# A row-packed two-head attention with 0/1 masks, and a circular convolution in half-length transforms, on one Trainium2 core

## The chip, the core and the metric

The kernel runs on one core of a Trainium2 chip. Its engines are TensorE (PE, whose weight loads are listed apart as PEld), VectorE (DVE), ScalarE (ACT), GpSimd (POOL) and SyncE (SP), which here only issues DMAs. Each engine runs its own instructions in order; semaphores tie them together. The metric is the device time of one launch in microseconds.

## The reference

Four batches, eight heads, 768 positions, 64 values a head. Three of the heads ("retrieval") see all earlier positions, the others only the first four positions and a window of 64. The output of all heads, 512 wide, goes through a gate: two projections multiply a third one that was convolved along the sequence (circularly, by FFT) with a filter given over time.

```python
scores = scale * np.matmul(q, k.transpose(0, 1, 3, 2))
stream_keep = causal & (is_sink | in_win)
mask = np.where(retr[0, :, 0, 0, None, None], full_mask, stream_mask)
scores = np.where(mask[None, :, :, :], scores, -1000000000.0)
a = np.exp(scores - np.max(scores, axis=-1, keepdims=True))
a = a / (np.sum(a, axis=-1, keepdims=True) + 1e-09)
x = np.matmul(a, v)                      # heads side by side: (B, S, 512)
proj = x @ w_proj                        # x1, x2, x3
X2 = np.fft.rfft(x2, n=S, axis=1)
H = np.fft.rfft(filter_fft, n=S, axis=0)[None, :, :]
x2_conv = np.fft.irfft(X2 * H, n=S, axis=1)
return (x1 * x2_conv * x3) @ w_out
```

## The kernel before

The work goes over 16 pairs of heads, four to a batch; the sequence is cut into six blocks of 128. `emit_loads` fetches q, k and v of a pair on SP's queue, two pairs ahead. `emit_prep` casts them to bf16 on DVE, transposes q and k on PE (L248, L250) and brings them back: q as two tiles qT_A and qT_B, each with one head's 64 rows and zeros in the other 64 (GpSimd memsets, L254 and L255), kT by a copy on ACT (L259).

`emit_attention` computes the scores transposed, keys down and queries across. For each head and key block a matmul of up to 512 columns fills one PSUM tile sc (four buffers; L275), a second one with the identity adds the mask to the first 256 columns (L284), and one exponential with a bias per head writes pT (L291). The value products (L306) take each 128x128 block of pT as weights against v with a column of ones, and DVE divides by that column (L313, L314). `flush_store` transposes the result into xT_all (L325, L327).

The gate of a batch is `emit_moe_proj` (x1 and x3, which are multiplied into g, L355 to L370; x2, L376, L382) and `emit_moe_fft`: a forward transform, a product with a 768x768 matrix G_all of cosines and sines (Xa L393, Xb L399), the complex product with the filter's transform Hp_all on DVE (L408 to L416), the inverse with G's transpose Minv_all (dps, L423), the product with g (L429), and the output projection (L434, copied on ACT, L441, stored on SP). Its PSUM tiles share two buffers.

G_all is built in twelve chunks by `emit_dft_chunk`, two in each of the first six pairs: angles on PE, their remainders on ACT and DVE, a sine on ACT (L220). Minv_all, six transposed tiles, is built in pairs 6 to 8, and Hp_all (`emit_hp`, L333, L339) after pair 8. The loop at the end writes prep of the next pair, one such step, attention, store and, after a batch's fourth pair, the gate; the first gate's transform waits until pair 8. The code order gives priorities only: a scheduler merges these streams on each engine by dependencies, buffers and its own estimate.

## Time and profile before

| | us |
|---|---|
| runs of the kernel, median of 3 | 390.17 (390.12 to 391.35) |
| span of the profiled execution | 390.7 |
| PE busy, share of the span | 298.7, 76% |
| ACT busy | 220.1, 56% |
| DVE busy | 177.3, 45% |
| POOL busy | 30.5, 8% |
| mean granted PE clock | 0.951 |

The profiled execution has no time of its own beside its span, which lies within the runs. Busy times of engines overlap, so none of them is the time by itself; a row of a group gives the mean of one instruction and, behind the second bar, how long its engine stood idle before it and whom it waited for. PE's mean includes the time in which a result is still on its way, so a dense run of matmuls is read from its length and count, not from the mean. A granted clock of 1.00 is 2.4 GHz, and the other level is 1.2 GHz; a figure between is a mix over the stretch.

### The profile page before, as it was taken

What the parts mean: (1) busy time and instruction counts of PE and PEld (TensorE: products, weight loads), DVE (VectorE), ACT (ScalarE), POOL (GpSimd) and SP (SyncE); (2) the same over time, 40 slices, a digit from 0 to 9 for tenths busy, and PEclk for the clock granted to TensorE, in tenths of its full rate; (3) what the DMA queues carried; (4) which work ended last, traced back from release to release, by engine and by line L of the source; (5) the groups of instructions that cost most, each with busy time, mean ns of one, the idle gap of its engine ahead of it and who ended that gap; (6) DMA issues with size and microseconds to landing.
All of it is one profiled execution on the core that took longest, in us unless ns stands there. A gap on an engine that the chain in (4) does not pass through costs nothing.

```text
span 390.7 us, 5920 instructions
## 1 busy us (share of the span) xinstructions
PE 298.7 (76%) x2257; PEld 176.7 (45%) x2288; DVE 177.3 (45%) x411; ACT 220.1 (56%) x409; POOL 30.5 (8%) x51
## 2 busy tenths in 40 slices
...
GB/s 148 198 197 225 83 154 59 81 42 120 2 122 3 29 94 49 124 112 81 3 41 2 81 169 114 2 168 75 2 0 2 1 142 23 0 2 0 0 2 161
DMA packets 80732, 28.44 MB, mean 73 GB/s; under 512 B 75840, under 2 KB 77120, under 8 KB 80704
## 3 DMA queue, kind: packets, MB, share of 16 engines
...
q14 instruction: 10, 0.08, 0.1%
...
## 4 chain that ended last, share of the span: by engine, by line
PE 51%; ACT 27%; DVE 7%; SPq 6%; DMA 4%; issue 4%; ACTq 0%; DVEq 0%
ACT pT L291 13%; PE dps L423 8%; PE sc L275 7%; PE x2p L376 5%; PE x3p L362 4%; ACT L291 4%; PE Xa L393 4%; ACT L220 4%; PE attout L306 4%; PE Xb L399 4%; PE x1p L355 3%; SPq L109 3%; PE ops L434 3%; DMA out_dram<-o_sb 3%; PE sc L284 3%
## 5 line engine op out<-in xcount | busy, mean ns | idle before, releaser
L291 ACT ACTIVATE pT<-sc,bias_all 128x512 bf16<-128x512 f32 (+3 forms) x256 | 120.2, 563 | 40.3 <-PE sc L284 24.6
L275 PE MATMUL sc<-qT_B,kT 128*128 128x512 bf16 (+3 forms) x128 | 41.1, 341 | 27.7 <-ACT pT L291 26.0
L306 PE MATMUL attout<-v_aug,pT 128*128 128x65 bf16 x672 | 54.0, 207 | 5.2 <-ACT pT L291 5.0
L306 PEld LDWEIGHTS <-pT 128*128 128x128 bf16 x672 | 41.8, 107 | 35.6 <-issue 19.2
L284 PE MATMUL sc<-mask_all,identity 128*128 128x256 bf16 x192 | 53.8, 290 | 0.3 <-DVE bias_all L171 0.2
L275 PE MATMUL sc<-qT_A,kT 128*128 128x128 bf16 (+3 forms) x126 | 38.3, 325 | 11.5 <-ACT pT L291 8.4
L259 ACT COPY kT<-kT_ps 128x768 bf16<-128x768 bf16 x16 | 12.8, 800 | 53.6 <-PE kT_ps L250 53.6
L313 DVE RECIPROCAL rec<-attout 128x6 f32<-128x6 f32 x32 | 6.2, 193 | 74.0 <-PE attout L306 73.9
L441 ACT COPY o_sb<-ops 128x512 f32<-128x512 f32 x24 | 14.0, 588 | 41.3 <-PE ops L434 27.0
L423 PE MATMUL dps<-Minv_all,P_all 128*128 128x512 bf16 (+1 forms) x188 | 34.8, 324 | 1.9 <-DVE m L411 0.6
L275 PEld LDWEIGHTS <-kT 128*128 128x128 bf16 x256 | 26.7, 105 | 19.2 <-issue 4.7
L284 PEld LDWEIGHTS <-identity 128*128 128x128 bf16 x192 | 19.5, 102 | 32.6 <-issue 29.3
L248 PE MATMUL qT_ps<-identity,q_bf 128*128 128x128 bf16 x96 | 14.1, 246 | 25.3 <-DVE q_bf L237 25.3
L370 DVE TENSOR_TENSOR g_all<-x1s,x3p 128x512 bf16<-128x512 bf16 (+1 forms) x32 | 17.7, 554 | 26.5 <-PE x3p L362 17.5
L355 PE MATMUL x1p<-xT_all,wproj_bf 128*128 128x256 bf16 (+1 forms) x120 | 25.6, 322 | 3.3 <-DVE xT_all L327 1.7
L362 PE MATMUL x3p<-xT_all,wproj_bf 128*128 128x256 bf16 (+1 forms) x123 | 26.2, 323 | 2.0 <-DVE g_all L370 1.5
L369 ACT CAST x1s<-x1p 128x512 bf16<-128x512 f32 (+1 forms) x32 | 15.3, 479 | 18.9 <-PE x1p L355 18.8
L423 PEld LDWEIGHTS <-P_all 128*128 128x128 bf16 x192 | 18.4, 97 | 15.9 <-issue 2.7
L254 POOL MEMSET qT_A<- 64x768 bf16 x16 | 12.1, 757 | 169.2 <-PE sc L284 136.9
L429 DVE TENSOR_TENSOR y_all<-g_all,dps 128x512 bf16<-128x512 bf16 (+1 forms) x32 | 17.0, 554 | 14.2 <-PE dps L423 14.2
L434 PE MATMUL ops<-wout_bf,y_all 128*128 128x512 bf16 x93 | 21.8, 378 | 1.1 <-ACT o_sb L441 0.8
L376 PE MATMUL x2p<-wproj_bf,xT_all 128*128 128x512 bf16 x93 | 21.3, 379 | 0.2
...
## 6 DMA issues: line engine op xcount, KB each, us to landing
...
ret_i<-in_is_retrieval_dram SPq DMA_DIRECT2D x1, 8.0 KB, 3.8
```

Source lines behind the costliest of these rows:

```text
L220: nc.scalar.activation(out=G_all[:, tcn, a:b], in_=m2_f, func=AF.Sin, bias=sinb, scale=ETA)
L275: nc.tensor.matmul(sc, lhsT=kT[:, j * 128:(j + 1) * 128], rhs=qTh[:, j * 128 + a:j * 128 + bb], start=True, stop=(a != 0),)
L284: nc.tensor.matmul(sc[:, 0:mw], lhsT=identity, rhs=mask_all[:, h, midx, 0:mw], start=False, stop=True,)
L291: nc.scalar.activation(out=pT, in_=sc, func=AF.Exp, bias=bias_all[:, bias_idx:bias_idx + 1], scale=SCALE,)
L306: nc.tensor.matmul(attout[:, i, :], lhsT=pt_pieces[hh][j][piece][:, qloc:qloc + 128], rhs=v_aug[:, j, 65 * hh:65 * hh + 65], start=(j == 0 ...
L355: nc.tensor.matmul(x1p, lhsT=wproj_bf[:, cc, cb * 128:(cb + 1) * 128], rhs=xT_all[:, b, cc, a:bb], start=(cc == 0), stop=(cc == NC - 1),)
L362: nc.tensor.matmul(x3p, lhsT=wproj_bf[:, cc, 2 * DM + cb * 128:2 * DM + (cb + 1) * 128], rhs=xT_all[:, b, cc, a:bb], start=(cc == 0), stop ...
L370: nc.vector.tensor_mul(g_all[:, cb, a:bb], x1s, x3p)
L376: nc.tensor.matmul(x2p, lhsT=xT_all[:, b, cc, ti * 128:(ti + 1) * 128], rhs=wproj_bf[:, cc, DM:2 * DM], start=(cc == 0), stop=(cc == NC - 1),)
L423: nc.tensor.matmul(dps, lhsT=P_all[:, rc, cb * 128:(cb + 1) * 128], rhs=Minv_all[:, rc, a:bb], start=(rc == 0), stop=(rc == NT - 1),)
L429: nc.vector.tensor_mul(y_all[:, cb, a:bb], g_all[:, cb, a:bb], dps)
L434: nc.tensor.matmul(ops, lhsT=y_all[:, cb, ti * 128:(ti + 1) * 128], rhs=wout_bf[:, cb, :], start=(cb == 0), stop=(cb == NC - 1),)
```

## The change

**Scores.** q stays one tile qT with head A in rows 0 to 63 and head B in rows 64 to 127, as kT. Each score matmul takes 64 rows, the two heads in turn, into two halves of one sc tile of 2x512 columns (two such buffers, four banks). The 21 blocks on and below the diagonal are packed into five chunks of four and one of one (CHUNKS), so that a pair has six exponentials over both heads, with no bias.

**Masks.** The identity matmuls go. DVE multiplies the first two blocks of each chunk (diagonal and the one beside it) by 0/1 masks after the exponential. The blocks farther off use v_far, a copy of v and its ones column multiplied by 0 or 1 per key and head on GpSimd.

**Convolution.** The sequence is folded, first half plus second and first minus second: even frequencies need only the sum, odd ones only the difference, so each transform has 384 points. G holds three such row blocks of six column groups; the last two groups take half a tile each for even and odd frequencies (64 output columns of the array forward, 64 rows back). Angles are computed without PE, and the three sines stand in one place. The inverse gives an even part ev and an odd part od; their sum and difference are the two halves.

**Order and buffers.** kT comes back on DVE. qT, kT, x and the gate's tiles all use ps_m with two buffers; att has one. The gate is a generator whose stages are emitted between the next batch's pairs, so batch 0's gate starts beside pair 5; all of batch 3's and the end of batch 2's come behind pair 15.

```diff
+CHUNKS = [
+    [(0, 0), (0, 1), (0, 2), (0, 3)],
+    [(4, 4), (4, 5), (0, 4), (0, 5)],
+    [(1, 1), (1, 2), (1, 3), (1, 4)],
+    [(3, 3), (3, 4), (3, 5), (1, 5)],
+    [(2, 2), (2, 3), (2, 4), (2, 5)],
+    [(5, 5)],
+]
+PLACE = {ji: 4 * c + n for c, blocks in enumerate(CHUNKS) for n, ji in enumerate(blocks)}
+NBLK = 21
...
+    asb = ctx.enter_context(tc.tile_pool(name="att_sb", bufs=2))
+    pTp = ctx.enter_context(tc.tile_pool(name="att_pT", bufs=2))
+    psw = ctx.enter_context(tc.tile_pool(name="ps_w", bufs=2, space=bass.MemoryType.PSUM))
+    pso = ctx.enter_context(tc.tile_pool(name="ps_o", bufs=1, space=bass.MemoryType.PSUM))
+    mps = ctx.enter_context(tc.tile_pool(name="ps_m", bufs=2, space=bass.MemoryType.PSUM))
...
-         tc.tile_pool(name="att_ps_w", bufs=4, space=bass.MemoryType.PSUM) as psw, \
-         tc.tile_pool(name="att_ps_o", bufs=2, space=bass.MemoryType.PSUM) as pso, \
-         tc.tile_pool(name="moe_ps", bufs=2, space=bass.MemoryType.PSUM) as mps:
...
+    for h in range(H):
+        nc.vector.scalar_tensor_tensor(
+            out=mask[:, h], in0=only, scalar=ret[:, h:h + 1], in1=stream,
+            op0=ALU.mult, op1=ALU.add,
+        )
+    vmask = const.tile([128, H, 2], FP32, name="vmask")
+    nc.vector.tensor_copy(out=vmask, in_=ret[:, :, None].to_broadcast([128, H, 2]))
+    if n_sink:
+        nc.vector.memset(vmask[0:n_sink, :, 0], 1.0)
...
+    G = const.tile([128, NM, 6, 128], BF16, name="G")
+    for m in range(NM):
+        e_t = setup.tile([128, 6, 128], FP32, name="e_t", bufs=2)
+        nc.vector.scalar_tensor_tensor(out=e_t, in0=fcol, scalar=tcol[:, m:m + 1], in1=off,
+                                       op0=ALU.mult, op1=ALU.add)
+        n_t = setup.tile([128, 6, 128], I32, name="n_t", bufs=2)
+        nc.vector.tensor_scalar(out=n_t, in0=e_t, scalar1=1.0 / S, scalar2=None, op0=ALU.mult)
+        nc.vector.scalar_tensor_tensor(out=e_t, in0=n_t, scalar=-float(S), in1=e_t,
+                                       op0=ALU.mult, op1=ALU.add)
+        nc.scalar.activation(out=G[:, m], in_=e_t, func=AF.Sin, scale=ETA)
+    Gi = const.tile([128, 6, HS], BF16, name="Gi")
+    def emit_inverse_matrix():
+        for t in range(0, 6, 2):
+            ps = mps.tile([128, 2, HS], BF16, name="gi_ps", tag="m")
+            for u in range(2):
+                for m in range(NM):
+                    nc.tensor.transpose(ps[:, u, m * 128:(m + 1) * 128], G[:, m, t + u, :], identity)
+            nc.vector.tensor_copy(out=Gi[:, t:t + 2, :], in_=ps)
...
+    def emit_forward(src, t, u):
+        ps = mps.tile([128, DM], FP32, name="X_ps", tag="m")
+        for m in range(NM):
+            first, last = m == 0, m == NM - 1
+            if t < 2:
+                nc.tensor.matmul(ps, lhsT=G[:, m, 2 * t + u, :], rhs=src[:, t, m, :],
+                                 start=first, stop=last)
+            else:
+                for r in range(2):
+                    nc.tensor.matmul(ps[64 * r:64 * r + 64, :],
+                                     lhsT=G[:, m, 4 + u, 64 * r:64 * r + 64],
+                                     rhs=src[:, r, m, :], start=first, stop=last)
+        return ps
...
+        fold = setup.tile([128, 2, NM, DM], BF16, name="fold")
+        nc.vector.tensor_add(fold[:, 0], filt[:, 0:NM, :], filt[:, NM:NT, :])
+        nc.vector.tensor_sub(fold[:, 1], filt[:, 0:NM, :], filt[:, NM:NT, :])
+        for t in range(3):
+            re = emit_forward(fold, t, 0)
+            for u in range(2):
+                nc.scalar.activation(out=HA[:, t, u, :], in_=re, func=AF.Copy, scale=2.0 / S)
+            if t == 0:
+                nc.scalar.activation(out=HA[0:1, 0, 0, :], in_=re[0:1, :], func=AF.Copy, scale=1.0 / S)
+            im = emit_forward(fold, t, 1)
+            for u in range(2):
+                nc.scalar.activation(out=HB[:, t, u, :], in_=im, func=AF.Copy,
+                                     scale=(2.0 if u else -2.0) / S)
...
-            nc.gpsimd.memset(qT_A[64:128, :], 0.0)
-            nc.gpsimd.memset(qT_B[0:64, :], 0.0)
-            nc.vector.tensor_copy(out=qT_A[0:64, :], in_=qT_ps[0:64, :])
-            nc.vector.tensor_copy(out=qT_B[64:128, :], in_=qT_ps[64:128, :])
-            kT = asb.tile([128, S], BF16, name="kT")
-            nc.scalar.copy(out=kT, in_=kT_ps)
...
+        v_far = asb.tile([128, 4, 2, 65], BF16, name="v_far")
+        for hh in range(2):
+            for j0, j1, n in ((0, 1, 0), (1, 4, 1)):
+                nc.gpsimd.tensor_scalar(
+                    out=v_far[:, j0:j1, hh, :], in0=v_aug[:, j0:j1, hh, :],
+                    scalar1=vmask[:, 2 * hp + hh, n:n + 1], scalar2=1.0,
+                    op0=ALU.mult, op1=ALU.mult)
+        turned = []
+        for name, src in (("q", q_f32), ("k", k_f32)):
+            bf = asb.tile([128, NT, 128], BF16, name=name + "_bf")
+            nc.vector.tensor_copy(out=bf, in_=src)
+            ps = mps.tile([128, S], BF16, name=name + "T_ps", tag="m")
+            for t in range(NT):
+                nc.tensor.transpose(ps[:, t * 128:(t + 1) * 128], bf[:, t, :], identity)
+            sb = asb.tile([128, S], BF16, name=name + "T")
+            nc.vector.tensor_copy(out=sb, in_=ps)
+            turned.append(sb)
...
-                        sc = psw.tile([128, w], FP32, name="sc", tag="w")
-                        nc.tensor.matmul(
-                            sc,
-                            lhsT=kT[:, j * 128:(j + 1) * 128],
-                            rhs=qTh[:, j * 128 + a:j * 128 + bb],
-                            start=True, stop=(a != 0),
-                        )
-                        if a == 0:
-                            mw = min(256, ncols)
-                            midx = 0 if j == 0 else 1
-                            nc.tensor.matmul(
-                                sc[:, 0:mw], lhsT=identity,
-                                rhs=mask_all[:, h, midx, 0:mw],
-                                start=False, stop=True,
-                            )
-                        pT = pTp.tile([128, w], BF16, name="pT", tag="p")
-                        bias_idx = 2 * h + 1 if j == 0 else 2 * h
...
+        pT = pTp.tile([128, 2, NBLK * 128], BF16, name="pT")
+        for c, blocks in enumerate(CHUNKS):
+            w = 128 * len(blocks)
+            sc = psw.tile([128, 2, 512], FP32, name="sc", tag="w")
+            for n, j, i, cnt in _runs(blocks):
+                for hh in range(2):
+                    rows = slice(64 * hh, 64 * hh + 64)
+                    nc.tensor.matmul(
+                        sc[:, hh, n * 128:(n + cnt) * 128],
+                        lhsT=kT[rows, j * 128:(j + 1) * 128],
+                        rhs=qT[rows, i * 128:(i + cnt) * 128],
+                        start=True, stop=True,
+                    )
+            nc.scalar.activation(out=pT[:, :, 512 * c:512 * c + w], in_=sc[:, :, 0:w],
+                                 func=AF.Exp, scale=SCALE)
+        h0 = 2 * hp
+        near = pT[:, :, 0:2560].rearrange("p hh (c w) -> p hh c w", w=512)
+        nc.vector.tensor_mul(near[:, :, 0, 0:256], near[:, :, 0, 0:256], mask[:, h0:h0 + 2, 0, :])
+        for c in range(1, 5, 2):
+            nc.vector.tensor_mul(
+                near[:, :, c:c + 2, 0:256], near[:, :, c:c + 2, 0:256],
+                mask[:, h0:h0 + 2, 1, None, :].to_broadcast([128, 2, 2, 256]))
+        nc.vector.tensor_mul(pT[:, :, 2560:2688], pT[:, :, 2560:2688], mask[:, h0:h0 + 2, 1, 0:128])
...
+        att = pso.tile([128, 2, 512], FP32, name="att")
+        for hh in range(2):
+            for i in range(NT):
+                for j in range(i + 1):
+                    at = 128 * PLACE[(j, i)]
+                    nc.tensor.matmul(
+                        att[:, hh, 65 * i:65 * i + 65],
+                        lhsT=pT[:, hh, at:at + 128],
+                        rhs=(v_far if i >= j + 2 else v_aug)[:, j, hh, :],
+                        start=(j == 0), stop=(j == i),
+                    )
...
-                nc.vector.tensor_mul(m1, Xa, Hp_all[:, i, :])
-                nc.vector.tensor_mul(m2, Xb, Hp_all[:, i1, :])
-                nc.vector.tensor_mul(m3, Xa, Hp_all[:, i1, :])
-                nc.vector.tensor_mul(m4, Xb, Hp_all[:, i, :])
-                nc.vector.tensor_sub(P_all[:, i, :], m1, m2)
-                nc.vector.tensor_add(P_all[:, i1, :], m3, m4)
...
-                    for rc in range(NT):
-                        nc.tensor.matmul(
-                            dps,
-                            lhsT=P_all[:, rc, cb * 128:(cb + 1) * 128],
-                            rhs=Minv_all[:, rc, a:bb],
-                            start=(rc == 0), stop=(rc == NT - 1),
-                        )
-                    nc.vector.tensor_mul(y_all[:, cb, a:bb], g_all[:, cb, a:bb], dps)
...
+        xf = msb.tile([128, NC, 2, HS], BF16, name="xf")
+        nc.vector.tensor_add(xf[:, :, 0, :], xT[:, :, 0:HS], xT[:, :, HS:S])
+        nc.vector.tensor_sub(xf[:, :, 1, :], xT[:, :, 0:HS], xT[:, :, HS:S])
...
+        yield
+        P = msb.tile([128, 3, 2, DM], BF16, name="P")
+        for t in range(3):
+            X = msb2.tile([128, 2, DM], BF16, name="X")
+            for u in range(2):
+                ps = emit_forward(x2, t, u)
+                nc.scalar.copy(out=X[:, u, :], in_=ps)
+            m1 = msb2.tile([128, 2, DM], BF16, name="m1")
+            nc.vector.tensor_mul(m1, X, HA[:, t])
+            m2 = msb2.tile([128, 2, DM], BF16, name="m2")
+            nc.vector.tensor_mul(m2, X[:, ::-1, :], HB[:, t])
+            nc.vector.tensor_add(P[:, t], m1, m2)
+        yield
...
+        for cb in range(NC):
+            ch = slice(cb * 128, (cb + 1) * 128)
+            ev = mps.tile([128, HS], FP32, name="ev", tag="m")
+            od = mps.tile([128, HS], FP32, name="od", tag="m")
+            for r, ps in ((0, ev), (1, od)):
+                for u in range(2):
+                    nc.tensor.matmul(ps, lhsT=P[:, r, u, ch], rhs=Gi[:, 2 * r + u, :],
+                                     start=(u == 0), stop=False)
+            for u in range(2):
+                for r, ps in ((0, ev), (1, od)):
+                    rows = slice(64 * r, 64 * r + 64)
+                    nc.tensor.matmul(ps, lhsT=P[rows, 2, u, ch], rhs=Gi[rows, 4 + u, :],
+                                     start=False, stop=(u == 1))
+            evs = msb2.tile([128, HS], FP32, name="evs")
+            nc.scalar.copy(out=evs, in_=ev)
+            conv = msb2.tile([128, S], BF16, name="conv")
+            nc.vector.tensor_add(conv[:, 0:HS], evs, od)
+            nc.vector.tensor_sub(conv[:, HS:S], evs, od)
+            nc.vector.tensor_mul(y[:, cb, :], conv, g[:, cb, :])
+        yield
...
-            if pi_ < NT:
-                emit_dft_chunk(2 * pi_)
-                emit_dft_chunk(2 * pi_ + 1)
-            elif pi_ - NT < 3:
-                emit_minv(2 * (pi_ - NT))
-                emit_minv(2 * (pi_ - NT) + 1)
...
+        prep = preps.pop((b, hp))
+        pT = emit_scores(hp, prep)
+        if n + 1 < len(pairs):
+            preps[pairs[n + 1]] = emit_prep(*pairs[n + 1])
+        attn = emit_values(prep, pT)
+        emit_turn(attn, xT, hp)
+        if n == 0:
+            emit_inverse_matrix()
+        if n == 1:
+            emit_filter()
+        next(gate, None)
+        if hp % 2:
+            next(gate, None)
+        if hp == HP - 1:
+            for _ in gate:
+                pass
+            gate = moe(b, xT)
+    for _ in gate:
+        pass
```

The order on ACT where the first sines stand. Before (pair 0; L220 is the sine, L291 the exponential):

```order
L291 ACTIVATE pT<-sc,bias_all 128x512
L220 ACT_TABLE_LOAD
L220 ACTIVATE G_all<-m_f,sinb 128x512
L291 ACT_TABLE_LOAD
L291 ACTIVATE pT<-sc,bias_all 128x384
L220 ACT_TABLE_LOAD
L220 ACTIVATE G_all<-m_f,sinb 128x256
L291 ACT_TABLE_LOAD
L291 ACTIVATE pT<-sc,bias_all 128x256
```

After (the end of pair 1, the start of pair 2 and the filter's copies HA and HB):

```order
L264 ACTIVATE pT<-sc 128x2x512 x5
L264 ACTIVATE pT<-sc 128x2x128
L174 ACT_TABLE_LOAD
L174 ACTIVATE G<-e_t 128x768 x3
L264 ACT_TABLE_LOAD
L264 ACTIVATE pT<-sc 128x2x512
L212 ACTIVATE HA<-X_ps 128x512 x2
L214 ACTIVATE HA<-X_ps 1x512
```

Twelve sines between exponentials became three in a row, and the filter's copies now stand inside pair 2.

The order on DVE at the start. Before (q_f_105 and q_f_114 are the loads of q of pairs 0 and 1):

```order
L237 CAST q_bf<-q_f_105 128x768
L238 CAST k_bf<-k_f_106 128x768
L240 CAST v_aug<-v_f_107 128x2x6x64
L243 MEMSET v_aug 128x12
L256 COPY qT_A<-qT_ps 64x768
L257 COPY qT_B<-qT_ps 64x768
L237 CAST q_bf<-q_f_114 128x768
```

After (q_f_85 and q_f_94 are the same loads, k_f_97 the second pair's k):

```order
L240 CAST q_bf<-q_f_85 128x768
L240 CAST k_bf<-k_f_88 128x768
L227 CAST v_aug<-v_f_91 128x12x64
L240 CAST q_bf<-q_f_94 128x768
L245 COPY qT<-qT_ps 128x768
L240 CAST k_bf<-k_f_97 128x768
L245 COPY kT<-kT_ps 128x768
```

Pair 1's two casts moved ahead of pair 0's copies out of PSUM.

The order on ACT around a batch's output. Before (batch 0's output copies o_sb, beside pair 9):

```order
L291 ACTIVATE pT<-sc,bias_all 128x512
L441 COPY o_sb<-ops 128x512 x2
L291 ACTIVATE pT<-sc,bias_all 128x384
L441 COPY o_sb<-ops 128x512
L291 ACTIVATE pT<-sc,bias_all 128x256
L441 COPY o_sb<-ops 128x512
L291 ACTIVATE pT<-sc,bias_all 128x128
L441 COPY o_sb<-ops 128x512
```

After (pair 12, batch 1's inverse evs and output, batch 2's x2, which is printed as x_2564, and pair 13):

```order
L264 ACTIVATE pT<-sc 128x2x512 x5
L363 COPY evs<-ev 128x384 x2
L264 ACTIVATE pT<-sc 128x2x128
L363 COPY evs<-ev 128x384 x2
L375 COPY o_sb<-out_ps 128x512 x6
L317 CAST x_2564<-x_ps 128x512 x6
L264 ACTIVATE pT<-sc 128x2x512 x5
```

The output copies no longer stand between exponentials; all six, and six copies of x2, lie between two pairs.

## Rows read from the trace of the kernel before

**Rows 1.** Busy time by stretch: us, then PE, PEld, DVE, ACT, POOL, granted clock, DMA

```profile
72.00:90.00 18.00, 10.49 (x99) 7.27 (x97) 7.10 (x18) 15.28 (x25) 1.47 (x2) 0.80 0.30 66
...
205.00:271.00 66.00, 61.84 (x469) 36.12 (x475) 41.43 (x88) 30.68 (x63) 4.59 (x6) 1.00 0.31 85
271.00:340.00 69.00, 64.32 (x527) 38.77 (x533) 32.70 (x69) 41.57 (x88) 1.47 (x2) 1.00 0.09 29
340.00:391.00 51.00, 38.40 (x186) 18.57 (x187) 19.43 (x36) 10.75 (x20) 0.00 (x0) 0.96 0.09 31
```

**Rows 2.** Groups by form on ACT: shapes xcount, busy us, mean ns, idle before

```profile
L291 ACT ACTIVATE pT<-sc,bias_all 128x512 bf16<-128x512 f32 x96 | 67.7, 705 | 24.9 <-PE sc L284 15.5 <-PE attout L306 6.4 <-PE sc L275 2.1
...
L291 ACT ACTIVATE pT<-sc,bias_all 128x128 bf16<-128x128 f32 x64 | 25.3, 396 | 2.6 <-PE sc L284 2.2 <-PE sc L275 0.4
...
L220 ACT ACT_TABLE_LOAD x12 | 15.4, 1283 | 0.2
L291 ACT ACT_TABLE_LOAD x12 | 15.4, 1283 | 0.2
```

**Rows 3.** Timeline of ACT: start, us, line, shapes of the first, count

```profile
164.14 6.07 ACT L291 ACTIVATE pT<-sc,bias_all 128x512 bf16<-128x512 f32 x14 [0.26 <-PE sc L275]
```

**Rows 4.** Timeline of DVE at the start: the casts of q and k

```profile
22.06 0.56 DVE L237 CAST q_bf<-q_f 128x768 bf16<-128x768 f32 x1 [20.48 <-DMA q_f<-in_q_dram]
...
28.07 0.56 DVE L237 CAST q_bf<-q_f 128x768 bf16<-128x768 f32 x1 [0.89 <-DMA q_f<-in_q_dram]
28.93 0.56 DVE L238 CAST k_bf<-k_f 128x768 bf16<-128x768 f32 x1 [0.30 <-DMA k_f<-in_k_dram]
```

**Rows 5.** Timeline of ACT: the first exponential

```profile
32.91 0.69 ACT L291 ACTIVATE pT<-sc,bias_all 128x512 bf16<-128x512 f32 x1 [0.73 <-DVE bias_all L171]
```

**Rows 6.** Groups by form on DVE

```profile
L314 DVE TENSOR_TENSOR attn_bf<-attout,rec 128x384 bf16<-128x384 f32 x32 | 17.7, 554 | 0.6
...
L429 DVE TENSOR_TENSOR y_all<-g_all,dps 128x512 bf16<-128x512 bf16 x16 | 11.0, 689 | 14.2 <-PE dps L423 14.2
...
L257 DVE COPY qT_B<-qT_ps 64x768 bf16<-64x768 bf16 x16 | 9.0, 561 | 0.5
...
L176 DVE SCALAR_TENSOR_TENSOR mask_all<-d_j,ret_f,stream_j 128x256 bf16<-128x256 f32 x8 | 3.7, 466 | 0.0
```

**Rows 7.** Timeline of DVE: two bf16 products from SBUF, one behind the other

```profile
360.36 0.42 DVE L412 TENSOR_TENSOR P_all<-m,m 128x512 bf16<-128x512 bf16 x1
360.69 0.42 DVE L413 TENSOR_TENSOR P_all<-m,m 128x512 bf16<-128x512 bf16 x1
```

**Rows 8.** Timeline of PE: dense runs

```profile
221.22 2.11 PE L423 MATMUL dps<-Minv_all,P_all 128*128 128x512 bf16 x12
...
226.91 0.74 PE L306 MATMUL attout<-v_aug,pT 128*128 128x65 bf16 x19
```

**Rows 9.** Timeline of the last gate: x1s copies, first output products, fifth output copy

```profile
345.91 0.59 ACT L369 CAST x1s<-x1p 128x512 bf16<-128x512 f32 x1 [1.50 <-PE x1p L355]
...
349.08 0.59 ACT L369 CAST x1s<-x1p 128x512 bf16<-128x512 f32 x1 [1.50 <-PE x1p L355]
...
379.49 3.61 PE L434 MATMUL ops<-wout_bf,y_all 128*128 128x512 bf16 x16
...
386.04 0.59 ACT L441 COPY o_sb<-ops 128x512 f32<-128x512 f32 x1 [1.31 <-DMA out_dram<-o_sb]
```

**Rows 10.** Timeline of ACT: the kT copy of pair 9

```profile
172.90 0.80 ACT L259 COPY kT<-kT_ps 128x768 bf16<-128x768 bf16 x1 [2.69 <-PE kT_ps L250]
```

**Rows 11.** Timeline of PE: two transposes, then a matmul on one row

```profile
89.86 0.22 PE L248 MATMUL qT_ps<-identity,q_bf 128*128 128x128 bf16 x1
89.92 0.22 PE L250 MATMUL kT_ps<-identity,k_bf 128*128 128x128 bf16 x1
90.07 0.39 PE L201 MATMUL e_ps<-fr_row,t_row 1*128 1x512 f16 x1
```

**Rows 12.** Timeline of PE: six products of 512 columns at either clock

```profile
363.54 2.65 PE L399 MATMUL Xb<-x_nat,G_all 128*128 128x512 bf16 x6
366.03 1.46 PE L393 MATMUL Xa<-x_nat,G_all 128*128 128x512 bf16 x6
```

478 lines of the change are left out of this document (139 added, 339 removed).

## The prediction

> **What bounds the kernel now.** I read the stretches first [rows 1]. From 72 to 90 us, a pair of heads of batch 0, ACT is busy 15.28 of 18.00 us while PE is busy 10.49 and the granted clock is 0.80; from 205 to 340 us PE is busy 126 of 135 at a clock of 1.00; after 340 us no attention is left and one batch's gate runs alone, 51 us with PE busy 38.4. So three bounds follow one another: ACT, then PE, then a chain. The groups of ACT say what its part is [rows 2]: 24 table loads of 1283 ns between exponentials and sines, 30.8 us, and the exponentials. All these loads lie in pairs 0 to 5, where the angles are built.
>
> **Prices.** An exp of 512 columns takes 705 ns, one of 128 takes 396 [rows 2]: 0.805 ns a column. Fourteen of them, 4608 columns, ran without a gap in 6.07 us [rows 3], which leaves (6.07 - 3.71) / 14 = 0.17 us each beside the columns. On VectorE 384 columns from PSUM take 554 ns and 512 take 689 [rows 6], 1.05 ns a column and 0.15 fixed; 512 bf16 columns from SBUF take 0.42 and the next starts 0.33 later [rows 7]. That gives 0.52 ns a column there and 0.09 less for each one that follows at once. On PE six products of 512 and six of 256 columns take 2.11 us, nineteen value products 0.74 [rows 8], so about 0.21 us for 512 columns and 0.04 for a value product.
>
> **The change, part by part.**
> Exponentials: a pair now has 16 in 5376 columns, 4.33 + 16 x 0.17 = 7.0 us; after it has six, 4.33 + 6 x 0.17 = 5.3 us. Over 16 pairs ACT loses 27 us. The sines now stand in one run of three, so two of those 24 loads are left: 28 us less on ACT in pairs 0 to 5. The copies of kT (0.80 each, on ACT) become VectorE copies, near 0.56 [rows 6].
> Masks: the 192 mask matmuls on PE go, 1.2 us a pair. In their place VectorE multiplies pT by 0 and 1: one product of 512 columns, two of 1024, one of 256, so 0.33 + 2 x 0.60 + 0.19 = 1.7 us a pair at the SBUF rate, or 3.2 at the PSUM rate, its other bound. I take 1.7, since P_all's product has these types [rows 7]. This is the added wait: the value products wait for it, and behind them on PE stand the next pair's scores, for which ACT then waits. The order shows c0 and most of c1 (the first two of a pair's six score blocks) ahead of these products and the rest behind. So after its last long exp a pair costs ACT about 2.2 us (mask 0.7, 37 value products 1.6, fill of a block 0.3, less the exponentials already fed).
> Masked copies of v: four GpSimd products a pair in place of two memsets of 0.73 to 0.76 each. Nothing in the trace multiplies there; by the memset's rate about 1 us, hidden because the copies belong to the next pair; at three times that they still end before the exponentials that they run beside.
> Row-packed scores: the same 16 matmuls a pair, each on half of the rows. If two run together, the streams of a pair fall from 2.3 to 1.1 us of PE; if not, they stay. I take the saving, but it hides behind exponentials, except for about 0.2 us a pair.
> Transforms: a batch's forward has 12 products of 512 columns and 12 of half width in place of 36, the inverse 16 full and 16 half-row products of 384 columns in place of 24 + 24 of 512 and 256. PE loses 7.7 + 7.7 - 5.1 - 5.1 = 5 us a batch. Against that ACT gains 6 copies of X and 4 of ev, VectorE gains two folds of 1536 columns. Each PSUM tile of the gate holds one of two buffers, and qT, kT and x now share those two. The loads and stores on SP's queue keep their sizes and number; each load still goes two pairs ahead, so I cost them at nothing.
>
> **The sum**, along the order after.
> 1. To the first exp: q of pair 0 is cast at 22.06 [rows 4], but the order puts pair 1's casts ahead of pair 0's copies from PSUM; those land at 28.07 and 28.93. Then 0.56 + 0.56 and a fill: 31 us, against 32.91 now [rows 5].
> 2. Pairs 0 and 1 take ACT 10.6 us, but VectorE then builds masks and angles: 8 mask products of 512 at 0.67 (256 columns take 466 ns [rows 6]), nine angle operations of 768 at about 0.73, two pairs' masks 3.4, two outputs 2, Gi 1.4, and the third pair's casts and copies 2.4, with waits some 24 us from 33. Pair 2 starts at 57.5.
> 3. Pair 2 has 14 filter copies (0.6 each) between its first exp and its second: 1 + 1.5 (fold) + 8.3 + 4.3 = 15. To 72.5.
> 4. Pairs 3 and 4 at 5.3 + 2.2: 15. To 87.5. Pair 5 with six x2 tiles, four products of 0.21 each: 12.5. To 100.
> 5. Pairs 6 and 7 with forward and gate: PE has 2 x 4.3 + 5.1 + 10.2 = 24. With two buffers, three products of 512 (0.64) before each copy of 0.59, it can't be dense: 28.5. To 128.5.
> 6. Pair 8: exponentials 4.2 until the inverse begins. The inverse with pair 8's products on VectorE (8 x 0.47 sums, 4 x 0.47 y, two folds 1.7, masks 0.8, xT 0.5) is 9 and with hand-overs 10.5. Output tiles at the pace of the last ones now, 7 us to the fifth copy [rows 9], turns 1.5, x2 5.5. The order puts pair 9's scores behind all that: 28.7. To 157.2.
> 7. Pairs 9 to 12 repeat it: 5.3 + 29.5 + 28.7 = 63.5. To 220.7. Pairs 13 to 15: 35. To 255.7.
> 8. The tail, where two gates wait: value products and turn 5, inverse of batch 2 9.5, output 7, x2 5.3, forward 5.5, gate 4 x 3.17 = 12.7 (from 345.91 to 349.08 is one of four now), inverse 9, output to the end 11.2 (from 379.49 to 390.7) [rows 9]: 65.2.
> Sum **321 us**, to be set against the profiled span of 390.7. The median is 390.17, so I take nothing off. Differences under 0.3% count as no change.
>
> The gain lies in the first half: pair 8 starts at 128.5 where it now starts near 173, behind pair 9's kT copy [rows 10]. From there on the work on PE falls by a third, but the time hardly, since the order after is more serial.
>
> **The rivals.**
> *Denser than that.* The three engines interleave better than my hand-overs allow, and a block of four pairs and a gate costs PE's own 47 us, not 63.5. For it: PE ran 94% busy from 205 to 340 with the same two buffers. Against: each tile's copy is now nearly as long as its products. 321 - 2 x 16.5 = 288.
> *Tile shapes cost what they should save.* The order has 196 changes between full, half-row and half-column matmuls, and 15 of the 128 score pairs are split by other work. A one-row matmul after transposes starts 0.15 us later where 0.055 is usual [rows 11]: 196 x 0.095 = 19. If the halves also run one after the other, 16 x 1.1 = 18 more. With seven tenths on the path: 347.
> The Trainium skill, TensorEngine Tiling (Array Packing), Key Properties, says that changing the tiling mode drains the engine. If each drain cost the 0.165 us by which a transpose outlasts its slot [rows 11], the 196 would be 32 us, an estimate, and that rival 356. No run here shows a drain.
> *Slower: the lower clock.* Batch 0 shows 0.80 where PE is busy 10.49 of 18 [rows 1], and with less work PE may spend the whole kernel so. Six products of 512 take 2.65 us at the lower level (1.2 GHz), 1.46 at the upper (2.4) [rows 12]. At the lower level throughout, 47 us of PE in a block become 92: a block of 100 instead of 63.5, and about 433 in all. It passes 391 when some six tenths of the time is at that level. Against: 340 to 391 us, PE busy three quarters, still had 0.96.
>
> **How the numbers follow.** Forecast 0.52 (301 to 341), denser 0.15, tile shapes 0.20, lower clock 0.07, something else 0.06 (a mask at the PSUM rate, +12, or slower GpSimd, mostly faster still). The range must leave out no more than 0.2: **286 to 356** takes in the forecast, most of the second and third. Faster 0.91, same 0.01, slower 0.08.
>
> **What would show it.** Exps of 2x512 near 1.1 us and three table loads; no exp from pair 1's end near 42 to about 57 us; a gap of some 14 us in the exponentials of ACT around each batch's output; mask products near 0.7 us for 1024; pair 8's first exp near 128. The step that I trust least is the serial pace in 5 and 6: if blocks of four pairs take under 52 us or over 75, the forecast falls with them. A clock under 0.8 over the second half would make all of it wrong.

## The result, and the profile after

The changed kernel takes 328.48 us (median of 4 runs, 326.54 to 329.73), the kernel before 390.5 in the runs beside it: a ratio of 0.840, with a 95% interval of 0.836 to 0.843. The profiled execution is the shortest of the four, 326.54 us, with a span of 324.8. From the page of it, busy time by engine and PE's granted clock in 40 slices of 8.1 us (tenths of 2.4 GHz):

```profile
span 324.8 us, 4957 instructions
...
PE 240.5 (74%) x1930; PEld 121.3 (37%) x1930; DVE 183.8 (57%) x353; ACT 157.1 (48%) x236; POOL 42.2 (13%) x97
...
PEclk9999999965999999999999999998999755999999
```

PE is busy 58 us less and ACT 63; DVE has gained 6.5. Groups on ACT, which answer to [rows 2] (mean ns of one behind the busy time; the first one mixes 80 exponentials of 1024 columns, 1032 ns each, with 16 of 256, 411 ns):

```profile
L264 ACT ACTIVATE pT<-sc 128x1024 bf16<-128x1024 f32 x96 | 82.4, 928 | 51.7 <-PE sc L258 51.7
...
L264 ACT ACT_TABLE_LOAD x2 | 2.6, 1283 | 8.7 <-PE sc L258 7.9 <-PEq L423 0.8
...
L174 ACT ACT_TABLE_LOAD x1 | 1.3, 1283 | 0.0
```

The timeline of ACT, in which L264 is the exponential (six make a pair) and L174 the sine; these are the rows at which the forecast's steps begin or end, and the last one holds pair 15's last three:

```profile
29.33 4.96 ACT L264 ACTIVATE pT<-sc 128x1024 bf16<-128x1024 f32 x6 [27.25 <-PE sc L258]
34.72 4.96 ACT L264 ACTIVATE pT<-sc 128x1024 bf16<-128x1024 f32 x6 [0.42 <-PE sc L258]
39.70 1.28 ACT L174 ACT_TABLE_LOAD   x1
...
57.18 1.02 ACT L264 ACTIVATE pT<-sc 128x1024 bf16<-128x1024 f32 x1
...
69.41 1.02 ACT L264 ACTIVATE pT<-sc 128x1024 bf16<-128x1024 f32 x1 [0.42 <-PE sc L258]
...
98.37 2.85 ACT L264 ACTIVATE pT<-sc 128x1024 bf16<-128x1024 f32 x3 [1.76 <-PE sc L258]
...
125.99 1.94 ACT L264 ACTIVATE pT<-sc 128x1024 bf16<-128x1024 f32 x2 [0.34 <-PE sc L258]
...
156.02 4.97 ACT L264 ACTIVATE pT<-sc 128x1024 bf16<-128x1024 f32 x6
...
219.33 4.97 ACT L264 ACTIVATE pT<-sc 128x1024 bf16<-128x1024 f32 x6
...
251.73 2.21 ACT L264 ACTIVATE pT<-sc 128x1024 bf16<-128x1024 f32 x3 [0.71 <-PE sc L258]
```

| step of the sum, its end | forecast | measured |
|---|---|---|
| 1 first exponential | 31 | 29.3 |
| 2 pair 2's first | 57.5 | 57.2 |
| 3 pair 3's first | 72.5 | 69.4 |
| 4 pair 6's first | 100 | 98.4 |
| 5 pair 8's first | 128.5 | 126.0 |
| 6 pair 9's first | 157.2 | 156.0 |
| 7 pair 13's first | 220.7 | 219.3 |
| 7 end of pair 15's exponentials | 255.7 | 253.9 |
| 8 end | 321 | 324.8 |

Up to the last exponential no step is off by more than 3 us; the tail is 70.9 us where 65.2 were forecast. Four stretches, which answer to [rows 1] (us, then PE, PEld, DVE, ACT, POOL, granted clock, DMA):

```profile
69.40:80.50 11.10, 9.94 (x117) 6.88 (x115) 6.61 (x16) 5.29 (x6) 1.75 (x6) 0.50 0.57 111
...
156.02:219.33 63.31, 53.23 (x475) 27.27 (x474) 40.90 (x79) 35.72 (x55) 7.54 (x20) 1.00 0.28 70
...
253.90:275.30 21.40, 17.75 (x83) 5.73 (x84) 10.47 (x19) 1.96 (x5) 0.00 (x0) 0.53 0.00 0
...
282.60:314.80 32.20, 29.45 (x149) 12.67 (x148) 16.15 (x29) 12.76 (x24) 0.00 (x0) 1.00 0.05 17
```

A cycle of four pairs and a gate takes 63.3 us with PE busy 53.2. PE is at the lower level, 1.2 GHz, from 69 to 80 us (pairs 3 and 4) and for 21 us after the last exponential, where batch 2's inverse and output lie; in the last gate, from 282.6 on, it is at the upper again.

A sum can come out right with wrong terms. So each run below undoes or adds one thing. The four runs of the kernel after lie 3.2 us apart, and the four of a kernel below up to 7.3, so a difference of 2 or 3 us from 328.5 is told from none only where the intervals of the ratios lie apart.

### The profile page after: what moved, and what is told of

The parts are those of the page before. It is cut to its first block, busy times and chain, and to the rows that moved or that the text cites. A ratio compares the mean times of both kernels' runs of the same rounds, so it can differ in the third digit from the quotient of the medians.

```text
span 324.8 us, 4957 instructions
## 1 busy us (share of the span) xinstructions
PE 240.5 (74%) x1930; PEld 121.3 (37%) x1930; DVE 183.8 (57%) x353; ACT 157.1 (48%) x236; POOL 42.2 (13%) x97
## 4 chain that ended last, share of the span: by engine, by line
PE 46%; DVE 19%; ACT 16%; SPq 7%; DMA 7%; issue 5%; ACTq 0%; DVEq 0%
ACT pT L264 8%; PE x3p L343 7%; SPq L90 7%; PE x_ps L314 7%; DMA out_dram<-o_sb 5%; PE x1p L337 5%; PE att L283 5%; PE sc L258 4%; PE X_ps L192 3%; PE od L355 3%; ACT o_sb L375 2%; PE od L360 2%; DVE pT L270 2%; PE out_ps L372 2%; PE x_ps L300 2%
## 5 line engine op out<-in xcount | busy, mean ns | idle before, releaser
L264 ACT ACTIVATE pT<-sc 128x1024 bf16<-128x1024 f32 x96 | 82.4, 928 | 51.7 <-PE sc L258 51.7
L258 PE MATMUL sc<-qT,kT 64*128 64x512 bf16 (+3 forms) x256 | 40.2, 344 | 22.2 <-ACT pT L264 16.9
L283 PE MATMUL att<-v_aug,pT 128*128 128x65 bf16 x352 | 34.4, 210 | 8.3 <-DVE pT L270 4.8
L233 POOL TENSOR_SCALAR v_far<-v_aug,vmask 128x65 bf16<-128x65 bf16 (+1 forms) x64 | 34.2, 553 | 46.5 <-DVE vmask L144 25.8
L372 PE MATMUL out_ps<-wout,y 128*128 128x512 bf16 x96 | 25.3, 399 | 6.2 <-ACT o_sb L375 5.3
L270 DVE TENSOR_TENSOR pT<-pT,mask 128x1024 bf16<-128x1024 bf16 x32 | 22.0, 689 | 12.2 <-ACT pT L264 12.2
L283 PE MATMUL att<-v_far,pT 128*128 128x65 bf16 x320 | 27.8, 211 | 0.0
L375 ACT COPY o_sb<-out_ps 128x512 f32<-128x512 f32 x24 | 13.6, 586 | 29.2 <-DMA out_dram<-o_sb 14.5
L343 PE MATMUL x3p<-xT,wproj 128*128 128x384 bf16 x128 | 26.1, 326 | 1.5 <-ACT x1s L340 0.8
L337 PE MATMUL x1p<-xT,wproj 128*128 128x384 bf16 x128 | 26.0, 325 | 0.0
L314 PE MATMUL x_ps<-wproj,xf 128*128 128x512 bf16 x96 | 21.6, 379 | 1.7 <-DVE kT L245 0.9
L363 ACT COPY evs<-ev 128x384 f32<-128x384 f32 x16 | 7.7, 481 | 29.9 <-PE ev L360 26.7
L317 ACT CAST x<-x_ps 128x512 bf16<-128x512 f32 x24 | 14.1, 585 | 11.0 <-PE x_ps L314 11.0
(78 smaller groups left out, 331.5 us busy)
```

The costliest lines, as they stand in the source:

```text
L233: nc.gpsimd.tensor_scalar(out=v_far[:, j0:j1, hh, :], in0=v_aug[:, j0:j1, hh, :], scalar1=vmask[:, 2 * hp + hh, n:n + 1], scalar2=1.0, op0 ...
L258: nc.tensor.matmul(sc[:, hh, n * 128:(n + cnt) * 128], lhsT=kT[rows, j * 128:(j + 1) * 128], rhs=qT[rows, i * 128:(i + cnt) * 128], start= ...
L264: nc.scalar.activation(out=pT[:, :, 512 * c:512 * c + w], in_=sc[:, :, 0:w], func=AF.Exp, scale=SCALE)
L270: nc.vector.tensor_mul(near[:, :, c:c + 2, 0:256], near[:, :, c:c + 2, 0:256], mask[:, h0:h0 + 2, 1, None, :].to_broadcast([128, 2, 2, 256]))
L283: nc.tensor.matmul(att[:, hh, 65 * i:65 * i + 65], lhsT=pT[:, hh, at:at + 128], rhs=(v_far if i >= j + 2 else v_aug)[:, j, hh, :], start=( ...
L314: nc.tensor.matmul(ps, lhsT=xf[:, cc, r, m * 128:(m + 1) * 128], rhs=wproj[:, cc, DM:2 * DM], start=(cc == 0), stop=(cc == NC - 1))
```

## The experiments

**The table loads alone, in the kernel before.** The angles go into G_all as whole numbers, and one sine at the end takes them all:

```diff
-            nc.vector.tensor_add(m2_f, m_f, c_f)
-            nc.scalar.activation(out=G_all[:, tcn, a:b], in_=m2_f, func=AF.Sin,
+            nc.vector.tensor_add(G_all[:, tcn, a:b].bitcast(FP16), m_f, c_f)
+            if ci == len(gchunks) - 1:
+                nc.scalar.activation(out=G_all, in_=G_all.bitcast(FP16), func=AF.Sin,
```

> The kernel before with one edit: the twelve sines become one activation over the whole matrix at the end of pair 5, so 22 of the 24 table loads go; nothing else moves. My theory (the table loads lie on the path, since ACT is the bound in pairs 0 to 5): 22 x 1.283 = 28 us less on ACT, the time falls to 360 to 366. Rival (the first half gained by the order, because the first gate stands beside pair 5 and not behind pair 8, and the loads filled time in which ACT waited anyway): 380 or more.

360.7 us (360.3 to 361.0), 0.922 of before (0.919 to 0.924). ACT's timeline, kT copies of pairs 2, 6 and 9, which mark the pairs:

```profile
48.10 0.80 ACT L259 COPY kT<-kT_ps 128x768 bf16<-128x768 bf16 x1 [1.18 <-PE kT_ps L250]
...
102.84 0.80 ACT L259 COPY kT<-kT_ps 128x768 bf16<-128x768 bf16 x1 [0.52 <-PE kT_ps L250]
...
143.03 0.80 ACT L259 COPY kT<-kT_ps 128x768 bf16<-128x768 bf16 x1 [2.69 <-PE kT_ps L250]
```

Pair 9's copy comes 29.9 us earlier than in [rows 10], and what follows it takes 216 us as it did (217.8). ACT is busy 31.5 us less up to that copy (85.7 in place of 117.2): 28.2 of table loads, the rest mostly one sine in place of twelve. PE's granted clock there rose too, from 0.90 to 0.95, but ACT's idle time did not fall (55.7 and 57.4), so the gain is ACT's. So about half of the change's 62 us is the single run of sines; 30.6 against 28.2 expected. The other half splits evenly: the kernel after reaches the same place, pair 8's first exponential, at 126.0, another 17 us earlier, and takes 198.8 from there to the end, 17 less. No run undoes the half-length transforms, so their part in this is not shown.

**More output buffers.**

```diff
-            o_sb = msb2.tile([128, DM], FP32, name="o_sb")
+            o_sb = msb2.tile([128, DM], FP32, name="o_sb", bufs=4)
```

> The kernel after with four buffers for the output copies o_sb in place of two (m1 and m2, which only VectorE touches, give up their second buffers for the room). My theory (a serial chain sets the pace in the output stage: product, copy, store, with the copy waiting for a store; 14.5 us of such waits in the trace after): each of the four output stages falls from 7.5 to about 5.3 us, the time from 328.5 to 318 to 322. Rival (TensorE sets the pace of the second half and the output stage is filled by other work): 326 to 329.

319.9 us (319.0 to 323.6), so 8.5 less. The group of the output copies on ACT in the kernel after; the last part is ACT's idle time ahead of them, and what ended it:

```profile
L375 ACT COPY o_sb<-out_ps 128x512 f32<-128x512 f32 x24 | 13.6, 586 | 29.2 <-DMA out_dram<-o_sb 14.5 <-PE out_ps L372 14.4
```

The same group with four buffers:

```profile
L375 ACT COPY o_sb<-out_ps 128x512 f32<-128x512 f32 x24 | 13.7, 586 | 21.7 <-PE out_ps L372 20.0 <-PE x_ps L314 1.2 <-PE qT_ps L243 0.6
```

The wait for the stores is gone and the copies follow one another at PE's pace, 0.86 us. The output stage was serial, as step 6 had it, and 8.5 of its 14.5 us of waits were on the path.

**No mask products.** L268 to L273 are left out, so the diagonal and the next blocks stay unmasked.

> The kernel after without the mask products on VectorE (left out: the masking of the diagonal and next-to-diagonal blocks; the masked copies of v stay). My theory (the value products wait for the masks, about 0.7 us a pair of the 2.2 that a pair costs beside its exponentials, and VectorE is the bound between pairs 1 and 2): 16 x 0.7 = 11 less, up to 3.4 more at pairs 0 and 1, so 314 to 320. Rival (the masks hide behind the next pair's exponentials as the row-packed scores do): 325 to 329.

318.0 us (316.8 to 320.9), 10.5 less, as many as expected, but not where. Pair 8 starts at 125.84, as with the masks, pair 13 at 214.28, 5.0 earlier. The exponentials end only 2.9 us earlier, after a stretch at 1.2 GHz from 220 to 228 us (in the kernel after mainly from 224 to 228). The tail is 7 us shorter, and its granted clock stays at 1.00 from 249 to 276 us. So the masks cost the pairs 3 to 5 us, not 11; the larger part lay in the tail. What idle time there does is a run of its own below.

**The weights later.** A small GpSimd copy from pair 0's k into each weight tile holds its load back until that k is there:

```diff
+    nc.gpsimd.tensor_copy(out=wproj[0:1, 0, 0:2], in_=loads[pairs[0]][1][0:1, 0, 63:65])
     nc.gpsimd.dma_start(out=wproj, in_=moe_w_proj.rearrange("(c p) n -> p c n", p=128))
```

> The kernel after with the three weight loads held on GpSimd's queue until k of pair 0 has landed. In the trace after, q of pair 0 is cast at 9.1 us, k only at 21.5, with the weights' 2.8 MB on the way beside it. My theory (the first exponential waits for loads only, and the weights delay them): the first exponential at 15 to 18 instead of 29.3 us, the time 314 to 319 if VectorE's set-up, which waits for a small load behind them on the same queue, comes as much earlier. Rival (the packets of q, k and v themselves set the pace, or the weights arrive too late for the filter): 325 or more.

327.1 us (326.3 to 327.9). The first exponential came at 10.09 us, 19 earlier, pair 2's only from 57.2 to 54.9. DVE's timeline where its set-up begins:

```profile
27.57 0.56 DVE L230 CAST v_aug<-v_f 128x768 bf16<-128x768 f32 x1 [13.42 <-DMA v_f<-in_v_dram]
28.42 0.17 DVE L118 TENSOR_SCALAR ret_w<-ret_i 128x16 f32<-128x16 int32 x1 [0.28 <-DMA ret_i<-in_is_retrieval_dram]
```

ACT's timeline, pair 0's exponentials and pair 2's first:

```profile
10.09 5.34 ACT L267 ACTIVATE pT<-sc 128x1024 bf16<-128x1024 f32 x6 [8.01 <-PE sc L261]
...
54.91 1.02 ACT L267 ACTIVATE pT<-sc 128x1024 bf16<-128x1024 f32 x1
```

My theory fell: step 1 of the forecast is not on the path at all. DVE's set-up waits for what now lands beside the weights.

**That, and is_retrieval first.** The small load moves ahead of q, k and v.

> As the run with the weights held back, and the small load of is_retrieval moved ahead of q, k and v on SP's queue. There the first exponential came at 10.1 us, 19 earlier, but the time fell by 1 only: VectorE began its set-up (masks, angles) at 28.4, behind the cast of pair 1's v at 27.6 and behind that small load, and pair 2's first exponential came at 54.9 against 57.2. My theory now (the path of the first 57 us goes through the set-up on VectorE, and through what it waits for): if the set-up starts at 14, pair 2 starts near 41 and the time is 312 to 315. If pair 1's v, which lands beside the weights, still holds VectorE until 27: 325 to 327. Rival (the first 57 us are ACT's): the first run would already have gained.

327.6 us (323.1 to 329.6): the second of the two cases. The cast of pair 1's v still starts at 28.39, and the set-up behind it.

**The set-up early.** Now the weights wait for pair 1's v (`loads[pairs[1]][2]` in the copies).

> The weights held back until pair 1's v has landed (not only pair 0's k), and the small load of is_retrieval first on SP's queue. With k alone as the condition the set-up on VectorE still stood behind the cast of pair 1's v at 28.4 us, and the time stayed at 327.6. My theory (the path of the first 57 us is: loads, then 26 us of VectorE set-up, then pair 2): the set-up begins at 8 to 10 and pair 2's first exponential comes at 36 to 42 instead of 57.2; the time is 309 to 315. Rival (the filter, which now arrives later, holds pair 2 or the gates as long): 322 or more.

326.3 us (325.0 to 329.2), not told from the kernel after: my theory fell again. DVE had its set-up done at 23.5 us. Then it stood, in its own order, before pair 3's q, which landed beside the weights; most of pair 0's mask products are behind that cast:

```profile
25.13 0.54 DVE L243 CAST k_bf<-k_f 128x768 bf16<-128x768 f32 x1
40.84 0.56 DVE L243 CAST q_bf<-q_f 128x768 bf16<-128x768 f32 x1 [15.17 <-DMA q_f<-in_q_dram]
```

Pair 2 began at 54.93 and pair 8 5.2 us earlier than in the kernel after, of which 2.2 were left at the last exponential. In the kernel after, the first 40 us have the DMA engines busy all the time (share 1.04, 190 GB/s). So I read the start as bound by loads: whichever step on DVE needs the load that comes last waits for it. The last run below bears this out in part.

**Row packing undone.** q goes into tiles with zeros in the other head's rows:

```diff
-                        lhsT=kT[rows, j * 128:(j + 1) * 128],
-                        rhs=qT[rows, i * 128:(i + cnt) * 128],
+                        lhsT=kT[:, j * 128:(j + 1) * 128],
+                        rhs=qT[:, hh, i * 128:(i + cnt) * 128],
```

> The kernel after with the row packing undone: q goes into tiles with zeros in the other head's 64 rows (zeroed once), each score product takes all 128 rows; m1 and m2 give up their second buffers for the room. My theory (two halves run together: in the trace after a pair of 512 columns is followed after 0.32 us, and the saving hides mostly): TensorE gains 1.1 us a pair, 0.2 to 0.5 of it on the path, VectorE one copy of 0.56 a pair: 331 to 340. Rival (the changes between tile shapes cost more than the packing saves): 326 or less.

339.3 us (334.7 to 339.7), 10.8 more. PE's timeline in the kernel after, a pair of score products of 512 columns, packed:

```profile
157.10 0.39 PE L258 MATMUL sc<-qT,kT 64*128 64x512 bf16 x2 [0.34 <-ACT pT L264]
```

The same pair in this run, on full rows:

```profile
167.35 0.59 PE L267 MATMUL sc<-qz,kT 128*128 128x512 bf16 x2 [0.28 <-ACT pT L273]
```

The 0.20 us between them is one product of 512 columns: the packed halves do run together. From pair 9's first exponential to pair 12's it took 34.7 us in place of 33.7, 0.3 a pair, as expected. But in this build the scheduler put DVE's set-up ahead of the first scores: the first exponential came at 44.2, pair 8 started 9.6 us later. The tail, on the other hand, is 4.9 us shorter, at 2.4 GHz through its inverse, where the kernel after is at 1.2. So the 10.8 is not the packing's price; 0.3 a pair, by estimate some 5 us in 16 pairs, is what the rows bear out.

**The inverse on full rows.** A copy of Gi with zeros in the other half makes the four 64-row products of an output block full ones, of the same columns:

```diff
-                    nc.tensor.matmul(ps, lhsT=P[rows, 2, u, ch], rhs=Gi[rows, 4 + u, :],
+                    nc.tensor.matmul(ps, lhsT=P[:, 2, u, ch], rhs=GiZ[:, r, u, :],
```

> The kernel after with the 64-row products of the inverse (two of four in each part) made over 128 rows, against a copy of Gi with zeros in the other half; m1 and m2 give up their second buffers for the room. The columns stay the same, so only the changes of the tile's shape go. My theory (changes of shape cost nothing on the path): 327 to 330. Rival (they do): in the trace after four products of 384 columns take 0.70 us in x1p, and two take 0.43 in the inverse; 32 x 0.04 = 1.3 us a batch, in a stretch in which TensorE is busy 9.6 of 10.2 us: 322 to 324.

325.4 us (322.3 to 329.5), 0.829 of before (0.824 to 0.834, below the 0.836 at which the interval of the kernel after begins). PE's timeline in the kernel after, two full products of the inverse and two of 64 rows:

```profile
134.14 0.50 PE L355 MATMUL ev<-Gi,P 128*128 128x384 bf16 x2
134.57 0.50 PE L360 MATMUL ev<-Gi,P 64*128 64x384 bf16 x2
```

The same place in this run (L366 in place of the 64-row products):

```profile
134.14 0.49 PE L366 MATMUL od<-GiZ,P 128*128 128x384 bf16 x2
134.46 0.49 PE L362 MATMUL ev<-Gi,P 128*128 128x384 bf16 x2
134.78 0.49 PE L366 MATMUL ev<-GiZ,P 128*128 128x384 bf16 x2
```

Two products take 0.43 us where the shape changes behind each two, and 0.32 where it doesn't: 0.1 us a change. (The two 64-row products of a pair stand on the same rows, so they don't run together; two of them cost what two full ones do.) There are 16 changes in an inverse, 1.7 us a batch. From its first evs copy to the first output copy, the inverse took 10.1, 9.2, 10.3 and 9.0 us in the four batches, against 10.2, 10.2, 15.6 and 9.7 in the kernel after. So 0.1 to 1.0 of the 1.7 showed where both are at 2.4 GHz. Batch 2's 5.3 are mostly the clock's: here too it fell behind the last exponential, but only from 263 to 270 us. The profiled execution is also the longest of the four, with other stretches at the lower level, so how much of the 3 us is the shapes' is not shown. My theory that changes of shape cost nothing fell in these rows; the rival was right in the price, and the time lies between the two.

**PE busy ahead of the tail.** Twelve products of 512 columns into att, ahead of pair 15's value products, which overwrite them:

```diff
+        for _ in range(idle):
+            nc.tensor.matmul(att[:, 0, :], lhsT=pT[:, 0, 1280:1408], rhs=wproj[:, 0, 0:512],
+                             start=True, stop=True)
```

> The kernel after with twelve extra products of 512 columns (2.6 us of TensorE, results overwritten) ahead of pair 15's value products. In the trace after TensorE stands idle from 251.8 to 254.4, waiting for the last exponentials and masks, the granted clock falls to 0.50 at 254.5 and stays there until 275.5, and the inverse of batch 2 takes 15.6 us from its first evs copy to the first output copy where it took 10.2 before. My theory (the idle time ahead of the tail brings the lower level, and that is the 5.7 us that the tail is longer than forecast): 322 to 325. Rival (the tail's own waits bring it anyway, or the extra products delay the values by as much): 327 to 330.

322.8 us (321.1 to 324.2), 5.7 less. In the kernel after, the stretch ahead of the tail (us, then PE, PEld, DVE, ACT, POOL, granted clock, DMA):

```profile
252.00:254.00 2.00, 0.39 (x7) 0.22 (x4) 0.49 (x2) 1.94 (x3) 0.00 (x0) 1.00 0.00 0
```

PE's timeline there, with its two waits, the second one for the masks (L270):

```profile
252.80 0.23 PE L258 MATMUL sc<-qT,kT 64*128 64x128 bf16 x2 [0.64 <-ACT pT L264]
254.45 0.20 PE L283 MATMUL att<-v_aug,pT 128*128 128x65 bf16 x1 [1.41 <-DVE pT L270]
```

Stretches of this run, which answer to the kernel after's 253.90 to 275.30 above:

```profile
256.00:262.00 6.00, 4.68 (x63) 2.61 (x61) 3.38 (x7) 0.48 (x1) 0.00 (x0) 1.00 0.00 0
262.00:270.00 8.00, 5.82 (x27) 1.77 (x26) 6.38 (x12) 1.44 (x3) 0.00 (x0) 1.00 0.01 2
270.00:276.00 6.00, 4.66 (x21) 1.92 (x21) 0.56 (x1) 2.25 (x4) 0.00 (x0) 1.00 0.36 133
```

The clock stays at 2.4 GHz, with no more work behind it than the kernel after has there, and the inverse takes 10.2 us from its first evs copy to the first output copy; the tail behind the last exponential takes 64.3 us in place of 70.9. So the longer tail is the clock's, and what brought it down was the wait before it, in which PE was not wholly idle: busy 0.39 of the 2 us from 252 to 254.

The other traces agree. In eight, the kernel after's among them, PE is busy 0.39 us of these 2 (in one 0.23), and in all eight the clock fell within 2 us behind the last exponential: for some 21 us in six of them, for 7 in two (the inverse on full rows, x2 one pair later). It did not fall there in the two runs with the extra products, nor without the masks (PE busy 0.67), nor with the row packing undone (0.55). It falls in other places too, in this run for parts of 148 to 168 us, where the kernel after keeps it; what brings it down there stays open.

**One exponential a head.** L264 in a loop over the two heads, twelve a pair.

> The kernel after with each exponential split in two, one for each head (twelve a pair). By the price of 0.17 us beside the columns ACT gains 6 x 0.17 = 1.0 us a pair. My theory (ACT is on the path in pairs 0 to 5 and, between its blocks, in one or two pairs of every four): 7 to 12 of the 16 us show, 335 to 340. Rival (TensorE and VectorE set the pace nearly everywhere after the change): 328 to 332.

333.0 us (330.8 to 334.9), 4.5 more. ACT's timeline: pair 9's exponentials and two more, without a gap:

```profile
156.20 6.58 ACT L265 ACTIVATE pT<-sc 128x512 bf16<-128x512 f32 x14
```

Pair 9's twelve took some 5.6 us where six took 4.97 in the kernel after, so an exponential costs near 0.1 us beside its columns and not 0.17. The 0.17 was read from exponentials with a bias operand ([rows 3]), and those of the kernel after have none; that this is the reason, no run shows by itself. ACT was busy 9.2 us more in all, 2.6 of it two more table loads ahead of pair 2, which still started at 57.4. Of this 4.5 showed, between theory and rival, and none of it before pair 9, which started at 156.2 (156.0 in the kernel after): ACT is not on the path there. The two-head exponential is worth 4 to 5 us here.

**x2 one pair later.**

```diff
-        next(gate, None)
+        if hp:
+            next(gate, None)
```

> The kernel after with the gate's first stage (x2) emitted one pair later, with the forward transform: the first scores of pairs 9 and 13 then stand ahead of x2 in place of behind it, and ACT's 22.5 us between pair 8's and pair 9's exponentials fall to about 15. My theory, the one of the forecast (the order after is serial, and a better mix shortens the block of four pairs and a gate from 63.5): 5 to 8 us in two blocks, 320 to 324. Rival (TensorE, busy 53 of 63.5 us in a block, is the bound with its hand-overs, wherever x2 stands): 326 to 331.

331.5 us (328.9 to 336.1); not told from the kernel after. In the profiled execution, the longest of the four, pair 9's scores do stand ahead of x2, but ACT's pause between pairs 8 and 9 went only from 22.5 to 20.5 us (131.0 to 151.5), at 2.4 GHz, with PE busy 16.1 of these. This other order of the same work gave nothing: my theory fell. That PE is the bound, as the rival says, is not shown by it, for the clock was at the lower level in parts of the cycle behind (0.92 in the mean, 1.00 in the kernel after).

**All that gained.** Four output buffers, the twelve products, the inverse on full rows, is_retrieval first, and the weights held back in the loop until pair 3's q has landed, the filter first:

```diff
+        if n == 1:
+            nc.gpsimd.tensor_copy(out=filt[0:1, 0, 0:2], in_=loads[pairs[3]][0][0:1, 0, 63:65])
+            nc.gpsimd.dma_start(out=filt, in_=moe_filter_fft.rearrange("(t p) c -> p t c", p=128))
```

> What gained alone, put together in the kernel after: four output buffers (8.5 us alone), twelve extra products ahead of the tail (5.7 alone), the inverse over 128 rows (3 alone); and the start in the order of need: is_retrieval first, the weights held back until pair 3's q has landed, the filter ahead of the other two. In the run with the set-up early, VectorE had done it by 23 us but then stood from 25.7 to 40.8 before the cast of a q that landed beside the weights, with pair 0's mask products behind that cast; here that q lands ahead of the weights. My theory (these are separate places on one path, so the gains add): pair 2's first exponential near 45 in place of 57.2, 328.5 - 8.5 - 5.7 - 3 - 12 = 299, so 295 to 303. Rival (one shared limit: the clock falls at another place as soon as one is mended, or TensorE's own work, 240 us busy, with its hand-overs leaves no more): 306 or more.

300.8 us (299.5 to 302.2), 0.768 of before (0.765 to 0.772), so 28 us below the kernel after. From its page:

```profile
span 300.2 us, 4986 instructions
...
PE 227.0 (76%) x1942; PEld 122.6 (41%) x1942; DVE 185.9 (62%) x355; ACT 159.4 (53%) x237; POOL 43.4 (14%) x101
...
PEclk9999999999999999999759899999999999999999
```

By the medians the gains add. The two profiles lie 24.6 us apart: pair 8's first exponential comes at 116.1, 9.9 earlier, the tail is 12.2 shorter, and 2.5 are gained between. So the steps at the start, which had given 1 to 2 us one by one, give about 10 here. The rival came true in part, too: from pair 9's first exponential to pair 13's it took 65.6 us at a mean granted clock of 0.90, where the kernel after took 63.3 at 1.00. The steps at the start are not at their end, for DVE still stands 8.6 us before the filter's fold with mask products behind it, and pair 2 starts at 50.2 where I expected 45.

## Why the prediction was right, and where it was not

**ACT first (right).** The run of sines was on the path in full: 30.6 us alone, and the gap between pairs 1 and 2 came as foreseen, 39.7 to 57.2.

**Step 1 and 2 (right numbers, part of the reason wrong).** The first exponential came at 29.3 as summed, but it is on no path: 19 us earlier, it moved the end by 1 at most. Step 2 counted 24 us of set-up on DVE from 33, and DVE is busy 23.1 of the 24.2 from 33 to 57.2, so the size is right; but when that work starts is set by loads. The prediction costed the loads at nothing since they keep their sizes and number. The sum did not show that this was wrong, because it took the start of the set-up from the old trace, and the loads landed much as there (pair 1's k is cast at 27.6, and at 28.9 before): the two steps came out right in part by luck.

**Exponentials and masks (sizes).** 0.17 us beside the columns was 0.1; a pair takes 4.97, not 5.3. The 1024-column mask product takes 0.69, a pair's masks 2.1 us of DVE where I took 1.7. Of the 0.7 us a pair on the path only 3 to 5 us in all showed directly; the wait for the masks did its harm at the tail, through the clock.

**GpSimd and row packing (right).** v_far takes 0.55 us a product, 2.2 a pair where I took about 1, and stays hidden: PE stood idle 0.0 us ahead of the products that read it. Packed halves run together, 0.20 us saved on a pair of 512 columns, mostly hidden.

**Steps 5 to 7 (right, the reason halved).** The cycle is 63.3 us, 63.5 forecast. The serial output stage is real. But PE is busy 53.2 of a cycle (with the time in which results are on their way) where I reckoned with 47, the changes of shape being one part of the difference (by estimate, 16 of 0.1 in the inverse); and moving x2 did not shorten it. So "serial" gave the right size; how much of the cycle PE's own work binds and how much its hand-overs is not shown.

**Tile shapes (the rival, right in its price).** The row of the one-row matmul gave 0.095 a change [rows 11], the runs 0.1. The rule that I set beside it (the Trainium skill, TensorEngine Tiling (Array Packing), Key Properties: a change of tiling mode drains the engine) agrees in direction; the estimate of 0.165 made from it was too much. The rival was wrong in two points: the halves do run together, and fewer than seven tenths of the changes lie on the path: for the inverse 0.1 to 1.0 us of 1.7 showed.

**Step 8 (wrong by 5.7 us).** The tail's terms for the inverse of batch 2, 9.5, and its output, 7, measured 14.1 and 9.6 (258.1 to 272.2, and on to x2 at 281.8); the others together were 1.5 too long. The same inverse for batch 3 took 8.4 at 2.4 GHz (304.2 to 312.5). The prediction had the lower clock as a rival for the whole kernel or not at all, at 0.07, and argued against it from a clock of 0.96 after 340 us before; it did not ask where PE would newly stand idle. That is the step that failed: the tail was summed with every product at 2.4 GHz. The change itself makes a place where PE stands idle, the wait of pair 15's value products for the masks; without the mask products the clock stayed up, and with them and PE kept busy it did too. With that, 322.8 remains, 2 us from the forecast.
